# Hash-bucket attention and a mixture of adapters on one core: prologue in another order, adapter work in one pair of heads, one more PSUM copy on ScalarE

## The chip, the cores and the metric

The kernel runs on one core of a Trainium2 chip, as one launch. The metric is the device time of one execution in microseconds (us). TensorE (PE in the rows; PEld is its weight load), VectorE (DVE), ScalarE (ACT), GpSimd (POOL) and SyncE (SP) each work through a queue of their own in order, and wait for one another by semaphores. DMAs are issued by SyncE, ScalarE and GpSimd.

## What is computed

```python
# q, k, v: (4, 8, 768, 64); proj: (64, 6); adapters: E = 8, r = 16; model width 512
q_bucket = sum over bits of ((q @ proj) > 0) * 2**bit      # k_bucket likewise
mask = q_bucket[..., :, None] == k_bucket[..., None, :]
attn = softmax(where(mask, q @ k.T / 8, -1e9))
x = (attn @ v)  arranged as (3072, 512)                    # a batch's 8 heads side by side
logits = x @ w_gate; the two largest per row, softmax over them -> w
out = x + sum over the two: w * ((x @ A[e]) @ B[e])
```

## The kernel before, in words

The 32 heads (4 batches of 8) go by *pairs*: 16 pairs, four to a batch. Partition p holds the six rows 6p to 6p+5 of a head. For a pair, `load` brings Q, K and V; `trans` transposes Q and K of both heads on TensorE in three groups of four 128x128 blocks (`tr{p}_0` to `tr{p}_2`), each followed by one copy out of PSUM into `qkT`; `hash` multiplies `qkT` by the hash vectors (`proj2`, made from the loaded `pst`), VectorE turns the result into signs (`sgn`), and four small DMAs (`sign_dma`) put the signs as six more rows under the casted Q and K in `aug`. So one matmul over 71 rows gives scores in which pairs of different buckets are pushed far down, and no mask is needed. `cast` (VectorE, two calls a pair) fills the other 64 rows of `aug`.

`run` goes through the pairs, and in each through nine *slots*. In slot s, `score` writes 1024 columns of scores into one of two PSUM buffers (pool `ps_s`, two buffers), and ScalarE takes their exponential into `P`. Behind the score each slot has other work on TensorE, written out by hand: probabilities times values (`pvmm`: the second head of the pair before in slots 1 to 3, the first head of this pair in slots 6 to 8), the transposes of coming pairs (group 2 of pair p+1 in slot 0, group 0 of pair p+2 in slot 3, group 1 of pair p+2 in slot 8), the hash of pair p+1 in slot 4, and `xtrans` in slot 7 (transposes of attention outputs `xb` for the adapters). `norm` (VectorE) divides by the sums, for the second head of the pair before in slot 3 and for the first head in slot 0 of the next pair, and frees the one PSUM buffer that `pvmm` writes into (`ps_v`). GpSimd casts V (`vcast`) and the attention outputs (`xb`). SyncE's queue has, per pair, the four sign DMAs (slot 4) and the loads of pair p+3 (slot 5) in this order.

Adapters of a batch start when its four pairs are done, in two halves of three row slots each (`moe_slot`, L432). Before the change a half takes two pairs: in slot 5 of the first the logits and the adapters' first product (`lgz`, TensorE, into the single buffer of `ps_m`) and the gate (`route`: on VectorE three maxima, the differences `d`, the mask `m`; on ScalarE their exponential `e`; on VectorE the weights `gw`, the product `zm`, the sum `ss` and its reciprocal `rt`); in slot 8 the transposes of `zm` and the copy `zmT` (`zmtrans`); and in slots 0, 2 and 3 of the next pair the three outputs (`delta`: one matmul `dl` of 512 columns into `ps_m`, and one VectorE operation that scales it by `rt` and adds `x`). The last half of batch 2 has its gate in pair 14 and its outputs in pair 15.

Pair 15 orders its columns by thirds (`third`), so that its own adapter work can start before all nine slots are done. Behind slot 8 comes the tail: the adapters of batch 3 in groups of two row slots. Every second output there is scaled by ScalarE into `tmp` and added by GpSimd (`split=True`), the others are done by VectorE.

`prologue` (L65) loads pair 0, warms TensorE with 36 matmuls on constants (`warm`), transposes pair 0 by four pieces `trf0` to `trf3`, hashes head 0 (`hsf0`) behind the second piece and head 1 (`hsf1`) behind the fourth, and sends the signs off. `pst` is loaded by two DMAs that ScalarE issues behind its two K loads.

## Time and profile before

| what | us |
|---|---|
| median of 3 runs (205.42 to 207.55) | 207.06 |
| the profiled execution | 207.07 |
| its span | 205.3 |
| ScalarE busy, 181 instructions | 157.3 (77%) |
| TensorE busy, 2177 matmuls | 177.2 (86%) |
| VectorE busy, 277 instructions | 124.7 (61%) |
| GpSimd busy, 107 instructions | 69.7 (34%) |

The span is the time between the first and the last instruction that the profile shows; the execution's time has 1.77 us around it. Busy shares are means over stages with different limits, so the windows of single stages are read beside them. In a row of the timeline the first number is the start, the second the length in us, then engine, line, operation, output and inputs, how often, and in brackets the idle time of the engine just before it and what ended it. Rows of one line that follow each other are merged, with their number behind the x.

### The profile page before, as it was taken

The numbers are of one execution on the slowest core, as the hardware profiler recorded it, in microseconds if no ns is written. First come the engines' busy times: TensorE is split into PE (matmuls) and PEld (weight loads), VectorE is DVE, ScalarE is ACT, GpSimd is POOL, SyncE is SP. The second block draws the span as 40 slices with busy tenths as digits, with TensorE's granted clock in tenths as the row PEclk, the third lists the DMA queues.
The fourth block names the chain that finished last, engine by engine and source line by source line (L and its number), as shares of the span: only waits on it lengthen the run. The fifth ranks groups of instructions, "written<-read, shape, count | busy, mean of one in ns | idle before, by whom it ended". The sixth has DMA issues, their size and how long they took to land.

```text
span 205.3 us, 5283 instructions
## 1 busy us (share of the span) xinstructions
PE 177.2 (86%) x2177; PEld 118.9 (58%) x2177; DVE 124.7 (61%) x277; ACT 157.3 (77%) x181; POOL 69.7 (34%) x107
## 2 busy tenths in 40 slices
...
GB/s 203 257 23 169 101 103 137 47 190 64 181 34 206 59 184 104 138 162 231 20 221 159 232 9 235 157 181 61 210 103 182 135 9 3 160 3 153 22 165 125
DMA packets 20984, 26.37 MB, mean 128 GB/s; under 512 B 6240, under 2 KB 19424, under 8 KB 20960
## 3 DMA queue, kind: packets, MB, share of 16 engines
...
q8 instruction: 17, 0.28, 0.5%
q14 instruction: 7, 0.06, 0.1%
HBM read 19.42 MB, written 6.29 MB: 125 GB/s over the span
## 4 chain that ended last, share of the span: by engine, by line
PE 50%; DVE 21%; issue 9%; ACT 7%; DMA 7%; SPq 2%; POOL 1%; ACTq 1%; POOLq 1%; DVEq 0%
PE s L273 19%; PE pv L280 10%; ACT P L275 6%; DVE qkT L209 6%; PE tr L202 5%; PE hs L222 5%; DVE aug L234 4%; DMA nat<-in_k_dram 4%; DVE x L308 4%; DVE acc L423 3%; DMA pst<-in_proj_dram 3%; PE xtp L348 3%; PE lz L363 2%; PE pv L289 2%; PE hsf L111 2%
## 5 line engine op out<-in xcount | busy, mean ns | idle before, releaser
L275 ACT ACTIVATE P<-s 128x1024 bf16<-128x1024 f32 x144 | 142.5, 1023 | 21.9 <-PE s L273 21.3
L273 PE MATMUL s<-aug 71*128 71x256 bf16 (+1 forms) x396 | 87.0, 326 | 1.0
L280 PEld LDWEIGHTS <-P 128*128 128x128 bf16 x1152 | 48.1, 98 | 11.5 <-issue 0.7
L273 PEld LDWEIGHTS <-aug 71*128 71x128 bf16 x396 | 34.4, 99 | 29.5 <-issue 18.7
L315 POOL CAST xb<-x 128x768 bf16<-128x768 f32 x15 | 12.4, 824 | 108.2 <-DVE x L308 108.2
L280 PE MATMUL pv<-vb,P 128*128 128x65 bf16 x1080 | 48.1, 195 | 0.0
L202 PE MATMUL tr<-ident,nat 128*128 128x128 f32 x180 | 29.0, 280 | 3.5 <-DMA nat<-in_q_dram 1.9
L209 DVE COPY qkT<-tr 128x512 f32<-128x512 f32 x31 | 21.2, 687 | 14.6 <-PE tr L202 14.5
L234 DVE TENSOR_SCALAR aug<-qkT 64x1536 bf16<-64x1536 f32 x30 | 28.6, 952 | 1.2
L202 PEld LDWEIGHTS tr<-ident,nat 128*128 128x128 f32 x180 | 19.9, 140 | 5.7 <-DMA nat<-in_k_dram 2.3
L354 DVE COPY xT<-xtp 128x768 bf16<-128x768 bf16 x15 | 8.4, 558 | 20.7 <-PE xtp L348 20.5
L308 DVE TENSOR_TENSOR x<-pv,ri 128x384 f32<-128x384 f32 x30 | 16.7, 557 | 1.2
L423 DVE SCALAR_TENSOR_TENSOR acc<-dl,rt,x 128x512 f32<-128x512 f32 x21 | 15.7, 745 | 2.5 <-PE dl L415 2.4
L225 DVE TENSOR_SCALAR sgn<-hs 128x384 bf16<-128x384 f32 x15 | 8.4, 558 | 14.1 <-PE hs L222 14.1
L186 POOL TENSOR_TENSOR vs<-vn 128x384 f32<-128x384 f32 x16 | 16.3, 1020 | 0.0
L184 POOL CAST vb<-vn 128x768 bf16<-128x768 f32 x16 | 13.4, 835 | 6.0 <-DMA vn<-in_v_dram 5.9
L415 PE MATMUL dl<-Bcat,zmT 128*128 128x512 bf16 x24 | 9.2, 401 | 5.4 <-DVE acc L423 4.9
L222 PE MATMUL hs<-qkT,proj 128*32 128x384 f32 x120 | 13.4, 521 | 0.0
L289 PE MATMUL pv<-vb,eps 128*128 128x390 bf16 x30 | 10.2, 342 | 2.3 <-DVE x L308 2.3
L207 ACT COPY qkT<-tr 128x512 f32<-128x512 f32 x14 | 8.1, 581 | 3.1 <-PE tr L202 3.1
L348 PE MATMUL xtp<-ident_bf,xb 128*128 128x128 bf16 x96 | 8.3, 219 | 2.5 <-DVE xb L336 1.9
L421 POOL TENSOR_TENSOR acc<-tmp,x 128x512 f32<-128x512 f32 x3 | 3.8, 1263 | 14.5 <-ACT tmp L420 14.5
...
## 6 DMA issues: line engine op xcount, KB each, us to landing
...
aug<-sgn SPq DMA_DIRECT2D x60, 9.0 KB
...
```

The lines of the kernel that those rows point to most:

```text
L186: nc.gpsimd.tensor_add(out=s3, in0=vn[:, :, 0:3, :], in1=vn[:, :, 3:6, :])
L202: nc.tensor.transpose(out=ps[:, j * P:(j + 1) * P], in_=self.nat[p][:, idx % 2, idx // 2, u * P:(u + 1) * P], identity=self.ident)
L209: nc.vector.tensor_copy(out=out, in_=ps)
L222: nc.tensor.matmul(out=ps[32 * j:32 * j + 32, :], lhsT=self.proj2, rhs=self.qkT[p][:, j * 384:(j + 1) * 384], start=True, stop=True)
L234: self.nc.vector.tensor_scalar(out=self.aug[p % 2][0:64, :, e * n:(e + 1) * n], in0=self.qkT[p][64 * e:64 * e + 64, :].rearrange("p (j c) ...
L273: nc.tensor.matmul(out=ps[:, o:o + n], lhsT=aug[0:71, 2 * h + 1, kt * P:(kt + 1) * P], rhs=q, start=True, stop=True)
L275: nc.scalar.activation(out=self.P_[p][:, s * 1024:(s + 1) * 1024], in_=ps, func=ACT.Exp, scale=128.0)
L280: self.nc.tensor.matmul(out=pv, lhsT=self.p_at(p, h, kt, i), rhs=self.vb[p % 3][:, h, self.slot(kt), :], start=False, stop=(last and kt == ...
L289: self.nc.tensor.matmul(out=self.pv[p, h], lhsT=self.eps, start=True, stop=False, rhs=self.vb[p % 3][:, h, self.T, :].unsqueeze(1).to_broa ...
L308: nc.vector.tensor_tensor(out=self.x[b][:, :, c:c + D].rearrange("p (u e) d -> p e u d", e=2), in0=pv[:, :, 0:D].rearrange("p (e u) d -> p ...
L348: nc.tensor.transpose(out=ps[:, i * P:(i + 1) * P], in_=self.xb[b][:, t, hp * P:(hp + 1) * P], identity=self.ident_bf)
L423: nc.vector.scalar_tensor_tensor(out=acc[:, i, :], in0=ps, scalar=rt, in1=x, op0=ALU.mult, op1=ALU.add)
```

## The change

- Prologue: `pst` is loaded by one DMA that reads `proj` twice, and is issued first on ScalarE's queue; the load of V of pair 0 goes behind the loads of pair 1. 38 warm matmuls, then all twelve transposes of pair 0 (into the two buffers of `ps_s`), five more warm matmuls, and then both hashes. All four sign DMAs are issued by SyncE. The first two groups of pair 1's transposes stand in the prologue, behind the hashes and ahead of the first score.
- In every pair the copy of transposes' group 2 (slot 0) is done by ScalarE and not by VectorE, so ScalarE has two such copies per pair (`on_act=True`).
- `moe_slot`: a half of a batch's adapters takes one pair: logits in slot 0, gate in slot 1, `zmtrans` in slot 3, the outputs in slots 5, 6 and 7. Pairs 5, 6, 9, 10, 13 and 14 carry a half each; the other pairs, and pair 15, none of earlier batches.
- Tail: all outputs by VectorE (no `split`), their matmuls into `ps_s`; `route` is cut in two (`route_a` up to `e`, `route_b` from `gw`) so that other work stands between them; two of the copies of `xT` go from ScalarE to VectorE.

```diff
     def prologue(self):
+
+        pst = sg.tile([P, 6], F32, name="pst")
+        nc.scalar.dma_start(out=pst, in_=self.proj.unsqueeze(0).to_broadcast([2, D, 6]))
-        self.load_v(0)
         self.load(1)
-
-        pst = sg.tile([P, 6], F32, name="pst")
-        for e in range(2):
-            nc.scalar.dma_start(out=pst[64 * e:64 * e + 64, :], in_=self.proj)
...
-        self.warm(36)
+        self.load_v(0)
+        self.warm(38)
+        for e in range(2):
+            nc.vector.tensor_copy(out=self.proj2[64 * e:64 * e + 64, e:12:2], in_=pst[64 * e:64 * e + 64, :])
         self.qkT[0] = self.qktp.tile([P, 2 * S], F32, tag="qkT", name="qkT0")
-        for j in range(4):
-            ps = self.ps_t.tile([P, 384], F32, tag="t", name=f"trf{j}")
-            for u in range(3):
...
-                h = j // 2
-                hs = self.ps_t.tile([P, 384], F32, tag="t", name=f"hsf{h}")
-                rows = slice(64 * h, 64 * h + 64)
-                for i in (2 * h, 2 * h + 1):
-                    nc.tensor.matmul(out=hs[32 * i:32 * i + 32, :], lhsT=self.proj2,
-                                     rhs=self.qkT[0][:, i * 384:(i + 1) * 384], start=True, stop=True)
-                sgn = self.sgp.tile([P, 384], BF16, tag="sgn", name=f"sgnf{h}")
...
-                for i in (2 * h, 2 * h + 1):
-                    self.sign_dma(nc.scalar if i == 1 else nc.sync, 0, i, sgn)
+        for h in range(2):
+            ps = self.ps_s.tile([P, 2, 512], F32, tag="s", name=f"trf{h}")
+            for i in range(2):
+                for u in range(3):
+                    nc.tensor.transpose(out=ps[:, i, u * P:(u + 1) * P],
+                                        in_=nat[:, i, h, u * P:(u + 1) * P], identity=self.ident)
+                out = self.qkT[0][:, (2 * h + i) * 384:(2 * h + i + 1) * 384]
+                (nc.scalar.copy if i else nc.vector.tensor_copy)(out=out, in_=ps[:, i, 0:384])
+        self.warm(5)
+        for h in range(2):
+            hs = self.ps_t.tile([P, 384], F32, tag="t", name=f"hsf{h}")
+            rows = slice(64 * h, 64 * h + 64)
+            for i in (2 * h, 2 * h + 1):
+                nc.tensor.matmul(out=hs[32 * i:32 * i + 32, :], lhsT=self.proj2,
+                                 rhs=self.qkT[0][:, i * 384:(i + 1) * 384], start=True, stop=True)
+            sgn = self.sgp.tile([P, 384], BF16, tag="sgn", name=f"sgnf{h}")
+            nc.vector.tensor_scalar(out=sgn[rows], in0=hs[rows], scalar1=0.0, scalar2=0.5,
+                                    op0=ALU.is_gt, op1=ALU.subtract)
+            for i in (2 * h, 2 * h + 1):
+                self.sign_dma(nc.sync, 0, i, sgn)
+            for e in range(2):
+                o = self.aug[0][0:64, 2 * h:2 * h + 2, e * 384:(e + 1) * 384]
+                i_ = self.qkT[0][64 * e:64 * e + 64, h * S:(h + 1) * S].rearrange("p (j c) -> p j c", j=2)
+                if e:
+                    nc.scalar.mul(o, i_, 2.0 ** -5)
+                else:
+                    nc.vector.tensor_scalar(out=o, in0=i_, scalar1=2.0 ** -5, scalar2=None, op0=ALU.mult)
+        self.trans(1, 0)
+        self.trans(1, 1, on_act=True)
...
-    def route(self, b, slots):
-        nc, P, E, r = self.nc, self.P, self.E, self.r
+    def route_a(self, b, slots):
...
         nc.scalar.activation(out=e, in_=d, func=ACT.Exp)
+        self.me[b, slots] = m, e
+
+    def route_b(self, b, slots):
+        nc, P, E, r = self.nc, self.P, self.E, self.r
+        lz, (m, e) = self.lz[b, slots], self.me[b, slots]
...
-        ps = (self.ps_t if last else self.ps_m).tile(
-            [P, self.Dm], F32, tag="t" if last else "m", name=f"dl{b}_{slots[i]}")
+        ps = (self.ps_s if last else self.ps_m).tile(
+            [P, self.Dm], F32, tag="s" if last else "m", name=f"dl{b}_{slots[i]}")
-        rt, x = self.rt[b, slots][:, i:i + 1], self.x[b][:, slots[i], :]
-        if split:
-            tmp = self.xp.tile([P, self.Dm], F32, tag="tmp", name=f"tmp{b}_{slots[i]}")
-            nc.scalar.activation(out=tmp, in_=ps, func=ACT.Copy, scale=rt)
-            nc.gpsimd.tensor_add(out=acc[:, i, :], in0=tmp, in1=x)
-        else:
-            nc.vector.scalar_tensor_tensor(out=acc[:, i, :], in0=ps, scalar=rt, in1=x,
-                                           op0=ALU.mult, op1=ALU.add)
+        nc.vector.scalar_tensor_tensor(out=acc[:, i, :], in0=ps, scalar=self.rt[b, slots][:, i:i + 1],
+                                       in1=self.x[b][:, slots[i], :], op0=ALU.mult, op1=ALU.add)
...
     def moe_slot(self, p, s):
-        for b in range(self.B - 1):
-            first = self.PPB * (b + 1) + 1
-            for g, (r, d) in enumerate(((first, first + 1), (first + 2, first + 3))):
-                if b == self.B - 2 and g == 1:
-                    r, d = r - 1, d - 1
-                slots = tuple(range(3 * g, 3 * g + 3))
-                if p == d and s in (0, 2, 3):
-                    self.delta(b, slots, (0, 2, 3).index(s))
-                if p == r:
-                    if s == 5:
-                        self.lgz(b, slots)
-                        self.route(b, slots)
-                    if s == 8:
-                        self.zmtrans(b, slots)
+        b, g = divmod(p - self.PPB - 1, self.PPB)
+        if b < 0 or b > self.B - 2 or g > 1:
+            return
+        slots = tuple(range(3 * g, 3 * g + 3))
+        if s == 0:
+            self.lgz(b, slots)
+        if s == 1:
+            self.route_a(b, slots)
+            self.route_b(b, slots)
+        if s == 3:
+            self.zmtrans(b, slots)
+        if s in (5, 6, 7):
+            self.delta(b, slots, s - 5)
...
                 if s == 0:
                     if p == 0:
                         self.load(2)
-                        self.trans(1, 0)
                     self.norm(p - 1, 0)
-                    if p > 0:
-                        self.trans(p + 1, 2)
+                    self.trans(p + 1, 2, on_act=True)
                 if s == 1:
                     if p == 0:
-                        self.trans(1, 1)
                         self.load_moe()
                     self.pvmm(p - 1, 1, 0, 2)
-                    if p > 0:
-                        self.cast(p + 1, 0)
+                    self.cast(p + 1, 0)
                     self.vcast(p + 1)
                 if s == 2:
-                    if p == 0:
-                        self.trans(1, 2)
-                        self.cast(1, 0)
                     self.pvmm(p - 1, 1, 2, 5)
                     self.cast(p + 1, 1)
                 if s == 3:
...
-                self.xtrans(p, t[0], last=True)
+                self.xtrans(p, t[0])
...
-                self.xtrans(p, t[1], last=True)
+                self.xtrans(p, t[1])
                 self.zmtrans(b, t[0], last=True)
                 self.third_x(1, self.x[b])
-            self.moe_slot(p, s)
         self.lgz(b, t[1])
-        self.route(b, t[1])
-        self.delta(b, t[0], 0, last=True, split=True)
+        self.route_a(b, t[1])
         self.third(2)
+        self.route_b(b, t[1])
+        self.delta(b, t[0], 0, last=True)
+        self.xtrans(p, t[2], on_act=True)
+        self.lgz(b, t[2])
+        self.zmtrans(b, t[1], last=True)
+        self.third_x(2, self.x[b])
+        self.route_a(b, t[2])
         self.delta(b, t[0], 1, last=True)
-        self.xtrans(p, t[2], last=True)
-        self.zmtrans(b, t[1], last=True)
-        self.lgz(b, t[2])
-        self.third_x(2, self.x[b])
-        self.delta(b, t[1], 0, last=True, split=True)
-        self.route(b, t[2])
+        self.route_b(b, t[2])
+        self.delta(b, t[1], 0, last=True)
+        self.zmtrans(b, t[2], last=True)
         self.delta(b, t[1], 1, last=True)
-        self.zmtrans(b, t[2], last=True)
-        self.delta(b, t[2], 0, last=True, split=True)
-        self.delta(b, t[2], 1, last=True)
+        for i in range(2):
+            self.delta(b, t[2], i, last=True)
```

Three places in the order of the queues. In the names of tiles the first number is the pair (`tr1_0`: pair 1, group 0; `s0_1`: pair 0, slot 1) or, for the adapters' tiles, batch and row slot.

TensorE in the prologue, behind its 36 warm matmuls, before:

```order
L95 MATMUL trf0_162<-ident_107,nat0_90 128x128 x3
L95 MATMUL trf1_169<-ident_107,nat0_90 128x128 x3
L111 MATMUL hsf0_174<-qkT0_161,proj2_112 32x384 x2
L95 MATMUL trf2_183<-ident_107,nat0_90 128x128 x3
L95 MATMUL trf3_188<-ident_107,nat0_90 128x128 x3
L111 MATMUL hsf1_193<-qkT0_161,proj2_112 32x384 x2
L273 LDWEIGHTS aug0_114
L273 MATMUL s0_0_222<-aug0_114 128x512
...
L202 MATMUL tr1_0_233<-ident_107,nat1_97 128x128 x4
```

and with the change, from the last of the first warm matmuls on (of the five others the first stands here):

```order
L153 MATMUL warm_123<-eps_102 128x128
L97 MATMUL trf0_165<-ident_104,nat0_92 128x128 x6
L97 MATMUL trf1_174<-ident_104,nat0_92 128x128 x6
L153 LDWEIGHTS eps_102
L153 MATMUL warm_183<-eps_102 128x128
...
L106 MATMUL hsf0_189<-qkT0_164,proj2_109 32x384 x2
L106 MATMUL hsf1_198<-qkT0_164,proj2_109 32x384 x2
L199 MATMUL tr1_0_208<-ident_104,nat1_97 128x128 x4
L199 MATMUL tr1_1_214<-ident_104,nat1_97 128x128 x4
L270 LDWEIGHTS aug0_111
L270 MATMUL s0_0_240<-aug0_111 128x512
...
L199 MATMUL tr1_2_250<-ident_104,nat1_97 128x128 x4
```

Both hashes have moved behind all transposes of pair 0, and `tr1_0` and `tr1_1` from behind the first scores to ahead of them.

ScalarE in pair 5, the first one with adapter work of batch 0, before:

```order
L275 ACTIVATE P5_1080<-s5_0_1081 128x1024
L275 ACTIVATE P5_1080<-s5_1_1098 128x1024
L275 ACTIVATE P5_1080<-s5_2_1123 128x1024
L275 ACTIVATE P5_1080<-s5_3_1147 128x1024
L207 COPY qkT7_1162<-tr7_0_1163 128x512
L275 ACTIVATE P5_1080<-s5_4_1169 128x1024
L275 ACTIVATE P5_1080<-s5_5_1184 128x1024
L383 ACTIVATE e0_0_1217<-d0_0_1213 128x24
L275 ACTIVATE P5_1080<-s5_6_1225 128x1024
```

and with the change:

```order
L272 ACTIVATE P5_1085<-s5_0_1086 128x1024
L204 COPY qkT6_987<-tr6_2_1097 128x512
L272 ACTIVATE P5_1085<-s5_1_1116 128x1024
L375 ACTIVATE e0_0_1149<-d0_0_1145 128x24
L272 ACTIVATE P5_1085<-s5_2_1159 128x1024
L272 ACTIVATE P5_1085<-s5_3_1183 128x1024
L204 COPY qkT7_1198<-tr7_0_1199 128x512
L272 ACTIVATE P5_1085<-s5_4_1212 128x1024
L272 ACTIVATE P5_1085<-s5_5_1227 128x1024
```

A second copy out of PSUM (`qkT6<-tr6_2`) stands behind exponential 0, and the gate's `e` has moved from behind exponential 5 to behind exponential 1.

VectorE from slot 7 of pair 5 to the last output of batch 0's first half in pair 6, before (`acc0_0` is the sum for row slots 0 to 2):

```order
L354 COPY xT1_1088<-xtp4_0_1260 128x768
L209 COPY qkT7_1162<-tr7_1_1285 128x512
L407 COPY zmT0_0_1295<-ztp0_0_1291 128x384
L306 RECIPROCAL ri5_0_1304<-pv5_0_1230 128x6
L308 TENSOR_TENSOR x1_1086<-pv5_0_1230,ri5_0_1304 128x2x3x64
L209 COPY qkT7_1162<-tr7_2_1307 128x512
L423 SCALAR_TENSOR_TENSOR acc0_0_1297<-dl0_0_1313,rt0_0_1208,x0_375 128x512
L234 TENSOR_SCALAR aug1_115<-qkT7_1162 64x4x384 x2
L423 SCALAR_TENSOR_TENSOR acc0_0_1297<-dl0_1_1365,rt0_0_1208,x0_375 128x512
L306 RECIPROCAL ri5_1_1379<-pv5_1_1320 128x6
L308 TENSOR_TENSOR x1_1086<-pv5_1_1320,ri5_1_1379 128x2x3x64
L423 SCALAR_TENSOR_TENSOR acc0_0_1297<-dl0_2_1390,rt0_0_1208,x0_375 128x512
```

and in pair 6 with the change, where the second half of batch 0 has gate and outputs in one pair:

```order
L231 TENSOR_SCALAR aug1_112<-qkT7_1198 64x4x384
L367 MAX top0_3_1366<-lz0_3_1328 128x8 x3
L369 TENSOR_TENSOR d0_3_1370<-lz0_3_1328,top0_3_1366 128x24
L372 TENSOR_TENSOR m0_3_1372<-lz0_3_1328,top0_3_1366 128x24
L385 TENSOR_TENSOR gw0_3_1378<-m0_3_1372,e0_3_1374 128x24
L386 TENSOR_TENSOR zm0_3_1376<-lz0_3_1328,gw0_3_1378 128x384
...
L231 TENSOR_SCALAR aug1_112<-qkT7_1198 64x4x384
...
L305 TENSOR_TENSOR x1_1091<-pv5_1_1345,ri5_1_1419 128x2x3x64
L407 COPY zmT0_3_1434<-ztp0_3_1430 128x384
L222 TENSOR_SCALAR sgn7_1446<-hs7_1441 128x384
L417 SCALAR_TENSOR_TENSOR acc0_3_1436<-dl0_3_1462,rt0_3_1377,x0_380 128x512
...
L347 COPY xT1_1093<-xtp5_0_1503 128x768
```

The gate stands between the two casts, the copy `zmT` ahead of the signs `sgn7`, and the sums `acc` behind them; the copy of `tr8_2` has left this queue.

## Rows read from the trace of the kernel before

**Rows 1.** Windows: busy PE, PEld, DVE, ACT, POOL, clock, DMA share, GB/s.

```profile
15.55:30.28 14.73, 12.11 (x91) 6.92 (x90) 6.01 (x9) 9.48 (x10) 5.70 (x8) 0.77 0.50 117
30.28:70.61 40.33, 38.47 (x499) 25.87 (x498) 22.67 (x41) 36.96 (x40) 13.94 (x20) 1.00 0.35 115
40.11:49.81 9.70, 9.42 (x127) 6.44 (x125) 5.63 (x11) 9.20 (x10) 3.47 (x5) 1.00 0.38 127
70.61:157.19 86.58, 81.71 (x1067) 56.27 (x1065) 60.66 (x133) 75.21 (x85) 27.76 (x40) 1.00 0.44 150
178.95:190.46 11.51, 9.30 (x145) 7.32 (x145) 7.00 (x21) 9.29 (x12) 0.83 (x1) 1.00 0.17 70
190.46:205.30 14.84, 4.87 (x52) 2.41 (x50) 6.65 (x22) 3.93 (x11) 3.79 (x3) 0.68 0.29 108
```

**Rows 2.** Timeline of the start, from the hash vectors to the first exponential.

```profile
1.68 1.19 ACTq L77 DMA_DIRECT2D pst<-in_proj_dram  x2
...
4.74 0.82 PE L95 MATMUL trf<-ident,nat 128*128 128x128 f32 x6
...
8.43 0.61 DVE L104 COPY proj<-pst 64x6 f32<-64x6 f32 x1 [1.63 <-DMA pst<-in_proj_dram]
...
9.19 1.49 PE L111 MATMUL hsf<-qkT,proj 128*32 128x384 f32 x4 [3.63 <-DVE proj L104]
...
10.73 0.55 DVE L114 TENSOR_SCALAR sgnf<-hsf 64x384 bf16<-64x384 f32 x1 [1.69 <-PE hsf L111]
...
11.31 1.64 ACTq L139 DMA_DIRECT2D aug<-sgnf  x1
...
14.91 0.33 PEld L273 LDWEIGHTS <-aug 71*128 71x128 bf16 x3 [1.20 <-DMA aug<-sgnf]
...
15.55 2.85 ACT L275 ACTIVATE P<-s 128x1024 bf16<-128x1024 f32 x3 [1.21 <-PE s L273]
```

**Rows 3.** Window of 1 us in the start, columns as in rows 1.

```profile
8.00:9.00 1.00, 0.00 (x0) 0.00 (x0) 0.57 (x1) 0.00 (x0) 1.00 (x2) 0.50 0.93 349
```

**Rows 4.** Timeline of pair 0, TensorE at the transposes of pair 2.

```profile
20.54 0.52 PE L202 MATMUL tr<-ident,nat 128*128 128x128 f32 x3 [1.89 <-DMA nat<-in_q_dram]
```

**Rows 5.** Chain of waits (start, us, what): a load of pair 2, logits in pair 9.

```profile
17.73 3.72 DMA nat<-in_k_dram
...
119.47 0.71 PE lz L363 x12
```

**Rows 6.** Timeline of an undisturbed pair, ScalarE, VectorE, TensorE at score 6.

```profile
40.11 1.94 ACT L275 ACTIVATE P<-s 128x1024 bf16<-128x1024 f32 x2 [0.31 <-PE s L273]
...
41.71 1.92 DVE L234 TENSOR_SCALAR aug<-qkT 64x1536 bf16<-64x1536 f32 x2
...
42.24 2.01 ACT L275 ACTIVATE P<-s 128x1024 bf16<-128x1024 f32 x2 [0.19 <-PE s L273]
...
44.15 0.58 ACT L207 COPY qkT<-tr 128x512 f32<-128x512 f32 x1
...
45.71 0.31 PEld L273 LDWEIGHTS <-aug 71*128 71x128 bf16 x2 [0.39 <-issue]
```

**Rows 7.** Timeline of pairs 9 and 10: gate and outputs of a half.

```profile
120.79 0.22 ACT L383 ACTIVATE e<-d 128x24 f32<-128x24 f32 x1 [0.26 <-DVE d L377]
...
122.01 0.18 DVE L392 RECIPROCAL rt<-ss 128x3 f32<-128x3 f32 x1
...
129.72 0.74 DVE L423 SCALAR_TENSOR_TENSOR acc<-dl,rt,x 128x512 f32<-128x512 f32 x1
```

**Rows 8.** Timeline of the tail.

```profile
192.03 0.18 DVE L385 TENSOR_TENSOR gw<-m,e 128x16 f32<-128x16 f32 x1 [0.20 <-ACT e L383]
...
196.21 1.26 POOL L421 TENSOR_TENSOR acc<-tmp,x 128x512 f32<-128x512 f32 x1 [2.29 <-ACT tmp L420]
196.27 1.23 DVE L385 TENSOR_TENSOR gw<-m,e 128x16 f32<-128x16 f32 x1 [0.67 <-ACT e L383]
...
200.39 1.26 POOL L421 TENSOR_TENSOR acc<-tmp,x 128x512 f32<-128x512 f32 x1 [2.92 <-ACT tmp L420]
```

51 lines of the change are left out of this document (15 added, 36 removed).

## The prediction

> **What bounds the kernel now.** I read the windows by stage first, then the timeline of each stage, and the chain of waits for what ends last in it. The windows [rows 1] split the run into a start (up to the first exponential at 15.55), pair 0, four pairs without adapter work, eight pairs with it, pairs 13 and 14 (157.19 to 178.95), the last pair, and a tail behind the last exponential. In an undisturbed pair (40.11 to 49.81) ScalarE is busy 9.20 of 9.70 us with nine exponentials and one copy, and TensorE 9.42: both are nearly full, and neither can be lengthened for nothing. The start and pair 0 are different: 15.55 and 14.73 us, with TensorE at a mean clock of 0.77 in pair 0. That is where idle time lies.
>
> The start [rows 2] is one chain. `pst`, the hash vectors, is issued last on ScalarE's queue (1.68); VectorE can take its second half only at 8.43; TensorE waits 3.63 us for it and then hashes the first head for 1.49 us; the signs are ready at 11.28 (10.73 + 0.55), their DMA lands for the score at 14.91, and the first exponential starts at 15.55. Meanwhile the clock has fallen to 1.2 GHz, half of full speed [rows 3], after TensorE had done nothing from 5.56 on. Pair 0 then waits 1.89 us for the Q rows of pair 2 [rows 4] and for its K rows until 21.45 [rows 5], since SyncE issues their loads only behind the signs (17.73).
>
> **The change, part by part.**
>
> *Start.* `pst` becomes the first DMA on its queue, 0.9 us ahead of its row in [rows 2], with no K rows in front. All twelve transposes stand behind 38 warm matmuls: 36 ended at 4.74, two more take 0.2; six transposes took 0.82, twelve take 1.65; five more warm matmuls 0.5. The hash starts near 7.1. At full clock the first head's 1.49 halves to 0.75, then 0.1 to VectorE and 0.55 for the signs: 8.6. From signs to score I keep what the rows show, 14.91 - 11.28 = 3.63, although both sign DMAs now stand on SyncE one behind the other (the row of ScalarE's has 1.64 for its issue alone, two on SyncE should be no more). Score at 12.2, first exponential 0.64 later, 12.85: a gain of 2.7. The two transposes of pair 1 that now stand ahead of the score lie in the 3.6 us in which it waits for signs; they cost nothing unless that wait gets shorter than about 1.2 us. V of pair 0 lands behind pair 1's rows now, about 2 us later, and GpSimd's casts and its DMAs of the adapters' weights with it; slot 6 of pair 0 is the first to need V, some 6 us behind the first score, so I cost that at nothing.
>
> *Pair 0.* Its bounds are the undisturbed 9.70 from below and 14.73 less the wait for Q, 12.8, from above. The load of pair 2 is issued behind the four signs, near 11.5 and 12.0; its K rows took 3.7 us [rows 5], so 15.7, and slot 3 needs them near 12.85 + 3.1: no slack, but no longer late by more than the wait that is there now. TensorE has little to do from about 8.8 to 12.2, as before the fall in [rows 3], so I expect 1.2 GHz for part of this pair. ScalarE hides most of that, since TensorE has no earlier pair's second half to do here. I take 10.8, nearer the lower bound. Pair 1 starts at 23.65 and not at 30.28: **-6.6**.
>
> *The second copy on ScalarE.* The transposes' third group is copied behind exponential 0, by ScalarE. VectorE's casts waited for VectorE's own copy and began at 41.71; they now wait for ScalarE's, which ends at the same point, 40.11 + 0.97 + 0.58 (two exponentials take 1.94, the copy that is there now 0.58 [rows 6]). So VectorE wins nothing on the path. ScalarE loses about 0.47: nine exponentials at 0.97 are 8.73, with the copy 9.20 [rows 1]. Of its two idle pieces, 0.31 ahead of exponential 0 and 0.19 ahead of exponential 2 [rows 6], the second is absorbed, so exponential 2 is 0.28 later. The first can't be: score 6 waits for the buffer that exponential 4 frees (45.71 [rows 6]), and from there it is 4.1 us to the next pair's first exponential (49.81), all of it TensorE's queue. The pair becomes 9.70 + 0.28, about 10.0. Bounds: 9.67 if both pieces vanish (9.20 + 0.47), 10.28 if neither does. The hash and its signs are late by the same 0.28, behind exponential 2. The first four pairs take 40.33 now, mean 10.08, 1.5 us in all over four undisturbed ones; at 10.0 to 10.3 each they cost 40.0 to 41.2. I take **+0.4**.
>
> *Adapters in one pair.* What two pairs shared (logits and gate in one, outputs in the next) stands in one; of each four pairs two carry it and two have none. TensorE's floor: the eight pairs have 81.71 busy, 10.21 each, against 9.42 without; 0.79 for a half, so 11.0 for both. Upwards, by the order on VectorE, counted from exponential 0: a cast (+1.6 to +2.56, half of the row of 1.92 in [rows 6]) stands ahead of the gate, whose head to `e` takes 0.61 (logits' end at 119.47 + 0.71 [rows 5] to 120.79 [rows 7]). So `e` starts at +3.1 to +3.2; ScalarE, ready for exponential 2 at +2.41, stops 0.65 and does `e`, with 0.13 net 0.78 late. In [rows 7] it stops 0.26 for the same thing. The logits (0.71) sit in the slack behind score 0. The first output waits for `zmT`: from `e` the gate takes 1.40 [rows 7], the other cast 0.96, the second normalisation and `zmT`'s copy about 1.1, so +6.5; exponential 4 ends at +6.6, so score 6 is no later for it. Two outputs stand behind score 6: 512 columns each, 0.22 by the logits' 1632 columns in 0.71, +0.44. Sum 10.0 + 0.78 + 0.44, about 11.2; I take 11.3. VectorE's three sums of 0.74 [rows 7] fit, but the signs are queued behind `zmT` (7.1, landing near 10.5, needed at 10.9): 0.4 of cover. If that is gone each adapter pair is longer by what it is late; upper bound 12.0. Four pairs: 2 x 11.3 + 2 x 10.0 = 42.6 against 43.29; twice: **-1.4**. Pairs 13 and 14 both carry adapters now: 11.3 + 10.85 (14 has one group of transposes less, 0.44) against 21.76: **+0.4**.
>
> *Last pair.* Three outputs of 0.22 leave TensorE's queue, for which ScalarE waits there (9.29 busy of 11.51 [rows 1]): **-0.6**.
>
> *Tail.* In [rows 8] a product of 16 elements takes 1.23 us and ends where GpSimd's addition ends (197.5); the one before it took 0.18. Without GpSimd's additions that is 1.05 back. VectorE now does all six outputs. Following its order from the last exponential's end: last third's values at +2.4, gate to +3.4, output +4.15, third +4.55, gate's head +5.15, output +5.9, gate +6.9, four outputs of 0.74 to +9.9; two copies of `xT` are among it and delay nothing that ends last; now the last addition ends at 201.65, +11.2 [rows 8]. **-1.3**; if TensorE's clock (a mean of 0.68 in the tail) delays the last two outputs, nothing is won.
>
> Sum: -6.6 + 0.4 - 1.4 + 0.4 - 0.6 - 1.3 = -9.1. The profiled execution took 207.07 (span 205.3), the median of the runs shown is 207.06. 207.07 - 9.1 = **198.0**.
>
> **Rivals.** *pst late (0.20).* In [rows 2] its second DMA took 6.1 us from its issue (2.3) to its use. If it takes that again it lands at 6.9, and VectorE's two `pst` copies stand ahead of its Q copies: Q is ready near 8.3, the hash 1.2 later, the K rows queued behind `pst` late as well, and TensorE idles longer, so pair 0 at 1.2 GHz: +1.3. Together 200.5. For it: the new DMA reads `proj` twice by a leading stride of zero. The Trainium skill, DMA: Bandwidth & Descriptors, Rules for kernel authors, says that a leading zero-stride broadcast of c copies confines a DMA to c engines, here two of sixteen; no run here shows it yet, and by that rule 200.5 would be the forecast. Against it: only 3 KB, and up to 6.0 it is covered.
>
> *Adapter pairs at 12.0 (0.16).* Signs or `zmT` late on VectorE: six pairs x 0.7 = 4.2, 202.2. For it: VectorE is busy some 8.9 of 11.3 in such a pair (5.63 plain, 60.66 / 8 with a half [rows 1], less the copy). Against it: 0.4 of cover.
>
> *Better (0.12).* Pair 0 at 10.0, and plain pairs at 9.7 (eight x 0.3): 194.8. For it: ScalarE is idle 0.5 in a plain pair. Against it: the chain from score 6.
>
> *Slower (0.05).* The clock falls inside the loop. ScalarE's longer pairs leave TensorE idle more. A pair of 9.42 busy would need 18.8 at 1.2 GHz, +9.1: one such pair ends the gain, one and a half give 211. Against it: the clock is 1.00 in all loop rows of [rows 1], in the last with TensorE busy 9.30 of 11.51.
>
> **How the numbers follow.** My forecast has 0.47, its own range 196 to 199.5. The range of 194.0 to 202.5 leaves out the slower case and the two middle ones together or past their prices. About 1% (2 us) is what a measurement of this kernel tells from no change. Faster by more: forecast, better, and each middle rival alone, less their joint cases, 0.89. Within 1%: late `pst` with long adapter pairs, 0.06. Slower: 0.05.
>
> **What would show it.** Right: the first exponential near 12.85; pair 1 near 23.6; one copy behind exponential 0, and pairs of 10.0 without adapter work, with no idle ahead of exponential 2; 11.3 in pairs 5, 6, 9, 10, 13; a wait of about 0.6 of ScalarE for `d`; no product over 0.3 in the tail. Wrong: VectorE waiting for `pst` past 6; scores waiting for signs in adapter pairs; a clock under 1.00 behind pair 1; first scores of pair 0 still waiting for pair 2's rows.

## The result, and the profile after

The changed kernel takes 199.19 us (median of 4 runs, 196.94 to 200.13) against 207.31 (205.42 to 207.86): a ratio of 0.9588, 95% interval 0.9476 to 0.9699. It is faster, by 8.1 us, and 1.2 us from the forecast of 198.0. Ratios here and below leave out executions more than 1.5% above the fastest of their kernel on that chip, so they are not the quotients of the medians, and the profiled execution of the change (200.13) is one of those left out. The sum behind the forecast, however, is wrong in almost every term. The profiled execution has a span of 198.0, 7.3 less than before; what it shows of the start holds for this execution, and p1_old_prologue below has the other three. By stages, in us, with starts read from ScalarE's timeline (in a merged row of exponentials the last one starts 1.02 ahead of the row's end):

| stage | before | after | change | forecast |
|---|---|---|---|---|
| start, to the first exponential | 15.55 | 16.62 | +1.07 | -2.7 |
| pair 0 | 14.73 | 14.74 | 0.0 | -3.9 |
| pairs 1 to 4 | 40.33 | 39.29 | -1.04 | +0.4 |
| pairs 5 to 12 | 86.58 | 83.31 | -3.27 | -1.4 |
| pairs 13, 14 | 21.71 | 21.66 | -0.05 | +0.4 |
| last pair | 11.56 | 10.56 | -1.0 | -0.6 |
| tail | 14.82 | 11.77 | -3.05 | -1.3 |

The windows of after, with the columns of [rows 1] and answering to them (start and pair 0; pairs 1 to 4; a pair without adapters; pairs 5 to 12; the last pair; the tail):

```profile
16.62:31.36 14.74, 14.06 (x83) 7.89 (x82) 3.15 (x4) 10.05 (x11) 9.22 (x12) 1.00 0.96 146
31.36:70.65 39.29, 37.96 (x499) 25.73 (x498) 20.20 (x37) 37.88 (x44) 13.85 (x20) 1.00 0.34 110
31.36:41.15 9.79, 9.45 (x127) 6.47 (x126) 5.11 (x10) 9.47 (x12) 3.47 (x5) 1.00 0.18 60
70.65:153.96 83.31, 81.27 (x1067) 55.89 (x1065) 55.62 (x125) 77.20 (x93) 27.78 (x40) 1.00 0.47 156
175.62:186.18 10.56, 8.57 (x142) 7.02 (x142) 4.91 (x19) 9.11 (x12) 0.83 (x1) 1.00 0.20 78
186.18:198.00 11.82, 5.30 (x52) 2.42 (x50) 7.93 (x27) 1.85 (x6) 0.00 (x0) 0.71 0.36 133
```

VectorE has 5 us less to do in pairs 5 to 12 (60.66 to 55.62), ScalarE 2 us more. In the first row the clock column reads 1.00, but this can't be so, as the rows of pair 0 below show: the trace's first record of the clock is at 30.7, and ahead of it the view fills in full speed.

The K loads of pair 0 on ScalarE's queue, before:

```profile
0.75 0.90 ACTq L71 DMA_DIRECT2D nat<-in_k_dram  x2
```

The start of after, from the issue of `pst` to the first exponential (timeline, answering to [rows 2]):

```profile
0.74 1.15 ACTq L69 DMA_DIRECT2D pst<-in_proj_dram  x1
...
1.92 0.84 ACTq L74 DMA_DIRECT2D nat<-in_k_dram  x2
...
4.08 1.46 DVE L91 COPY proj<-pst 64x6 f32<-64x6 f32 x2 [1.32 <-DMA pst<-in_proj_dram]
...
5.08 0.85 PE L97 MATMUL trf<-ident,nat 128*128 128x128 f32 x3
...
5.97 0.56 DVE L100 COPY qkT<-trf 128x384 f32<-128x384 f32 x1 [0.42 <-PE trf L97]
6.61 1.28 ACT L100 ACT_TABLE_LOAD   x1 [6.61 <-DVE qkT L100]
6.90 1.14 PEld L97 LDWEIGHTS trf<-ident,nat 128*128 128x128 f32 x6 [1.37 <-DVE qkT L100]
6.93 1.51 PE L97 MATMUL trf<-ident,nat 128*128 128x128 f32 x6 [1.00 <-DMA nat<-in_k_dram]
...
9.10 0.90 PE L97 MATMUL trf<-ident,nat 128*128 128x128 f32 x3 [0.65 <-DVE qkT L100]
...
10.46 1.59 PE L106 MATMUL hsf<-qkT,proj 128*32 128x384 f32 x8
...
12.61 3.37 SPq L136 DMA_DIRECT2D aug<-sgnf  x4
...
16.62 1.02 ACT L272 ACTIVATE P<-s 128x1024 bf16<-128x1024 f32 x1 [1.07 <-PE s L270]
```

`pst` is there by 4.08, so the hash no longer waits for it. But the twelve transposes don't run in a row. K's three wait for VectorE to have copied Q's three, since both lie in one PSUM tile (`trf0`, `trf1`), and for their rows, which are there at 6.93 only (before, the six transposes from 4.74 on had them without a wait): `pst`, 1.15 us to issue, now stands ahead of them on ScalarE's queue, so that they leave at 1.92 and not at 0.75. Of the fourteen traces of this document the six with the old order have no such wait, the eight with the new order all have one (0.67 to 2.40); what `pst` and the other loads that changed places each do to it was not tried. ScalarE's table load, which stood at 2.9 in the old order, now stands behind the same copy (6.61). And six transposes take 1.51 us, not 0.82. The hashes start at 10.46, where the prediction had 7.1.

Pair 0 of after on TensorE, and the same operation behind it (timeline):

```profile
21.48 0.48 PE L199 MATMUL tr<-ident,nat 128*128 128x128 f32 x1 [0.42 <-DMA nat<-in_k_dram]
...
22.73 1.51 PE L219 MATMUL hs<-qkT,proj 128*32 128x384 f32 x8
...
26.18 0.87 PE L277 MATMUL pv<-vb,P 128*128 128x65 bf16 x12
...
32.55 0.53 PE L277 MATMUL pv<-vb,P 128*128 128x65 bf16 x12
```

Twelve products take 0.87 us in pair 0 and 0.53 in pair 1, and the eight hash matmuls 1.51 against 0.85 (at 45.24): TensorE ran at 1.2 GHz through the start and pair 0, up to about 30 us, when the trace's first clock record says 1.00. K rows of pair 2 are still waited for (21.48).

ScalarE in a pair without adapters, and in pair 5, which holds a whole half (timeline of after, answering to [rows 6] and [rows 7]):

```profile
41.15 1.02 ACT L272 ACTIVATE P<-s 128x1024 bf16<-128x1024 f32 x1 [0.31 <-PE s L270]
...
42.07 0.58 ACT L204 COPY qkT<-tr 128x512 f32<-128x512 f32 x1
...
42.53 2.88 ACT L272 ACTIVATE P<-s 128x1024 bf16<-128x1024 f32 x3
...
45.25 0.63 ACT L204 COPY qkT<-tr 128x512 f32<-128x512 f32 x1
...
45.72 4.91 ACT L272 ACTIVATE P<-s 128x1024 bf16<-128x1024 f32 x5
...
73.61 0.22 ACT L375 ACTIVATE e<-d 128x24 f32<-128x24 f32 x1 [0.42 <-DVE d L369]
...
80.37 1.02 ACT L272 ACTIVATE P<-s 128x1024 bf16<-128x1024 f32 x1 [0.33 <-PE s L270]
```

The copy starts 0.92 behind exponential 0, whose row says 1.02, and exponential 1 starts 0.46 behind the copy, whose row says 0.58: what follows directly starts some 0.1 before the row ahead of it ends. The three exponentials take 2.72 up to the second copy. Exponential 4 starts 4.57 behind exponential 0; before it was 4.50 (40.11 to 44.61). The pair takes 9.79, the pair with a half 11.05.

The tail of after (timeline, answering to [rows 8]):

```profile
191.20 0.17 DVE L385 TENSOR_TENSOR gw<-m,e 128x16 f32<-128x16 f32 x1
...
192.02 2.90 DVE L417 SCALAR_TENSOR_TENSOR acc<-dl,rt,x 128x512 f32<-128x512 f32 x4
```

No product of 16 elements takes 1.23 us any more. The last output is written at 194.92, 8.74 behind the last exponential's end (before 11.2), and the span ends 3.0 later (before 3.65).

### The profile page after: what moved, and what is told of

It reads as the page before. It is cut to its first block, busy times and chain, and to the rows that moved or that the text cites. A ratio compares the mean times of both kernels' runs of the same rounds, so it can differ in the third digit from the quotient of the medians.

```text
span 198.0 us, 5277 instructions
## 1 busy us (share of the span) xinstructions
PE 180.7 (91%) x2184; PEld 122.2 (62%) x2184; DVE 116.5 (59%) x266; ACT 159.7 (81%) x192; POOL 66.8 (34%) x104
## 4 chain that ended last, share of the span: by engine, by line
PE 48%; DVE 20%; ACT 12%; DMA 7%; issue 6%; SPq 2%; ACTq 1%; POOLq 0%; POOL 0%; DVEq 0%
PE s L270 17%; PE pv L277 12%; ACT P L272 9%; DMA nat<-in_k_dram 7%; PE tr L199 6%; DVE aug L231 5%; ACT qkT L204 3%; DVE qkT L206 3%; DVE x L305 3%; PE pv L286 3%; PE xtp L345 3%; DVE zm L386 2%; PE dl L415 2%; DVE acc L417 2%; SPq L136 2%
## 5 line engine op out<-in xcount | busy, mean ns | idle before, releaser
L270 PE MATMUL s<-aug 71*128 71x256 bf16 (+1 forms) x396 | 89.9, 333 | 2.5 <-ACT P L272 1.8
L277 PEld LDWEIGHTS <-P 128*128 128x128 bf16 x1152 | 48.5, 99 | 11.6 <-issue 1.0
L199 PE MATMUL tr<-ident,nat 128*128 128x128 f32 x180 | 30.9, 294 | 1.1 <-DVE sgnf L109 0.6
L199 PEld LDWEIGHTS tr<-ident,nat 128*128 128x128 f32 x180 | 21.4, 149 | 4.0 <-DVE sgnf L109 2.3
L347 DVE COPY xT<-xtp 128x768 bf16<-128x768 bf16 (+1 forms) x17 | 8.9, 526 | 24.0 <-PE xtp L345 24.0
L204 ACT COPY qkT<-tr 128x512 f32<-128x512 f32 x30 | 17.9, 596 | 3.4 <-PE tr L199 3.4
L417 DVE SCALAR_TENSOR_TENSOR acc<-dl,rt,x 128x512 f32<-128x512 f32 x24 | 17.9, 748 | 2.9 <-PE dl L415 2.8
L206 DVE COPY qkT<-tr 128x512 f32<-128x512 f32 x15 | 10.4, 692 | 13.1 <-PE tr L199 13.1
L181 POOL CAST vb<-vn 128x768 bf16<-128x768 f32 x16 | 13.3, 830 | 5.5 <-DMA vn<-in_v_dram 4.9
L222 DVE TENSOR_SCALAR sgn<-hs 128x384 bf16<-128x384 f32 x15 | 8.3, 553 | 11.2 <-PE hs L219 11.2
L415 PE MATMUL dl<-Bcat,zmT 128*128 128x512 bf16 x24 | 9.8, 409 | 1.1 <-ACT zmT L405 0.2
L185 POOL TENSOR_TENSOR vs<-vs 128x128 f32<-128x128 f32 x16 | 7.6, 476 | 1.3
```

What stands on the lines that cost most here:

```text
L199: nc.tensor.transpose(out=ps[:, j * P:(j + 1) * P], in_=self.nat[p][:, idx % 2, idx // 2, u * P:(u + 1) * P], identity=self.ident)
L204: nc.scalar.copy(out=out, in_=ps)
L206: nc.vector.tensor_copy(out=out, in_=ps)
L270: nc.tensor.matmul(out=ps[:, o:o + n], lhsT=aug[0:71, 2 * h + 1, kt * P:(kt + 1) * P], rhs=q, start=True, stop=True)
L277: self.nc.tensor.matmul(out=pv, lhsT=self.p_at(p, h, kt, i), rhs=self.vb[p % 3][:, h, self.slot(kt), :], start=False, stop=(last and kt == ...
L417: nc.vector.scalar_tensor_tensor(out=acc[:, i, :], in0=ps, scalar=self.rt[b, slots][:, i:i + 1], in1=self.x[b][:, slots[i], :], op0=ALU.mu ...
```

## The experiments

**Theory:** the gain comes from the loop and the tail alone; the new prologue gives nothing, since its transposes wait for PSUM tiles and TensorE runs at 1.2 GHz. **Rival:** the prologue gives its 6.6 us and one unlucky profile hides it. Within the loop: either placement or ScalarE's copy carries the gain. The stages of each kernel's profiled execution, in us, read as above; the last column is the median of its runs, and in brackets that of the kernel before on the same chip:

| kernel | start | pair 0 | 1-4 | 5-12 | 13, 14 | last | tail | median |
|---|---|---|---|---|---|---|---|---|
| before | 15.55 | 14.73 | 40.33 | 86.58 | 21.71 | 11.56 | 14.82 | 207.31 |
| after | 16.62 | 14.74 | 39.29 | 83.31 | 21.66 | 10.56 | 11.77 | 199.19 (207.31) |
| p1_old_prologue | 14.79 | 14.88 | 39.20 | 83.31 | 21.67 | 10.56 | 11.92 | 199.60 (206.94) |
| p2_adapters | 14.49 | 16.51 | 39.42 | 83.86 | 21.87 | 10.92 | 15.61 | 203.39 (206.94) |
| p3_act_copy | 13.33 | 17.84 | 39.56 | 84.25 | 21.12 | 11.56 | 14.83 | 203.81 (206.94) |
| p4_tail | 13.68 | 16.88 | 39.36 | 87.29 | 21.73 | 11.21 | 11.70 | 203.63 (206.94) |
| p5_free | 15.47 | 13.56 | 39.14 | 84.24 | 22.07 | 10.56 | 11.74 | 197.46 (207.65) |
| p6_loads | 17.23 | 12.98 | 40.92 | 83.74 | 21.67 | 10.56 | 11.77 | 200.29 (207.65) |
| p7_keep | 15.25 | 15.05 | 39.43 | 91.54 | 22.42 | 10.56 | 11.74 | 204.53 (207.65) |
| p8_start | 13.88 | 9.46 | 40.67 | 86.42 | 22.34 | 10.56 | 11.76 | 199.10 (207.65) |
| p9_start_early | 13.81 | 9.46 | 39.16 | 83.34 | 21.67 | 10.56 | 11.99 | 192.10 (206.14) |
| p10_early | 15.49 | 14.28 | 39.15 | 83.32 | 21.67 | 10.56 | 11.88 | 197.70 (206.14) |
| p12_before_early | 15.05 | 14.78 | 38.92 | 86.17 | 21.72 | 11.56 | 14.84 | 205.60 (206.14) |
| p11_no_keep | 14.84 | 9.46 | 39.47 | 83.31 | 21.67 | 10.57 | 11.99 | 193.89 (206.51) |

Where no load is late, pairs 5 to 12 repeat within 0.05 us from kernel to kernel with the changed loop (83.31 to 83.34 in five traces) and within 0.4 with that of before (86.58 and 86.17), so what one part does there can be read from single traces. The start and pair 0 don't repeat: with one and the same prologue (before, p1 to p4) their sum lies between 29.67 and 31.18, the first exponential alone between 13.33 and 15.55. Single executions scatter more: those of the kernel before lie between 202.25 and 208.52 on one chip.

**p1_old_prologue**, the change without its prologue:

```diff
-        (prologue of the changed kernel; trans(1, 0) and trans(1, 1) in it)
+        (prologue of the kernel before; trans(1, 0..2) in slots 0, 1, 2 of pair 0)
```

> The changed kernel with the prologue of before and the transposes of pair 1 back in the slots of pair 0; all else as changed. Theory (the new prologue gives nothing: first exponential 16.62 against 15.55 us, pair 0 14.74 against 14.73): the first exponential starts at 15.5 to 15.6 us, exponential 0 of pair 1 at 30.3, and the time is about 1 us below the changed kernel's median of 199.2, so about 198.1. Rival (the new prologue does give its 6.6 us wherever TensorE runs at full speed early, and the profiled execution only did not show it): 203 to 205.5 us.

Measured: 199.60 us (198.1 to 200.42), ratio to before 0.9696 (0.9567 to 0.9825); first exponential 14.79, exponential 0 of pair 1 at 29.67. Everything behind that point takes 166.65 us, in the changed kernel 166.59. If that part is as long in the other runs, which no trace shows, their spans give their start and pair 0 as an estimate: 30.3, 32.0 and 32.0 here (spans 197.0, 198.6, 198.6), 28.2, 30.1 and 30.7 for the changed kernel (194.8, 196.7, 197.3). So in the mean of four (30.1 against 31.0) the new prologue gives 0.9 us, less than the runs scatter, and not 6.6. The rival, 203 us or more, falls; the theory's 198.1 isn't met either.

**p2_adapters, p3_act_copy, p4_tail**, each one part of the change in the kernel before:

```diff
 # p2_adapters: moe_slot of the changed kernel, none in the last pair
+        b, g = divmod(p - self.PPB - 1, self.PPB)
...
+        if s in (5, 6, 7):
+            self.delta(b, slots, s - 5)
 # p3_act_copy
-                        self.trans(p + 1, 2)
+                        self.trans(p + 1, 2, on_act=True)
 # p4_tail: xtrans, route_a / route_b, delta and the tail of the changed kernel
-        self.delta(b, t[0], 0, last=True, split=True)
+        self.route_a(b, t[1])
         self.third(2)
+        self.route_b(b, t[1])
+        self.delta(b, t[0], 0, last=True)
```

> The kernel before, with only the adapter outputs moved (a whole group in one pair, none in the last pair). Theory (by the stages, where the pairs without adapters already give 0.26 us each by the copy alone): pairs 5 to 12 lose 3.27 - 8 x 0.26 = 1.2 us, pairs 13 and 14 gain 0.45, the last pair loses 0.7: together -1.4, about 205.9 us from 207.3. Rival (the whole gain of pairs 5 to 12 and of the last pair is the placement's): -3.3 - 1.0 = -4.3, about 203.

> The kernel before, with only the third transposed piece of each pair from pair 1 on copied out of PSUM by ScalarE in place of VectorE. Theory (pairs 1 to 4 hold no adapters in either kernel and became 0.26 us shorter each): 14 pairs x 0.26 = -3.6, about 203.7 us from 207.3; the gap ahead of exponential 2 of a pair is gone, and 0.58 us of copy takes its place on ScalarE, overlapped so that exponential 4 starts at most 0.1 later. Rival (the term of the prediction: the copy costs about 0.1 us a pair more than it frees): 207.5 to 208.5.

> The kernel before, with only what the change does to the last pair's own adapters and behind the last exponential (no GpSimd additions, copies of xT on VectorE, the route in two halves, outputs from the two-bank PSUM pool); adapters of the batch before stay in the last pair. Theory (tail 14.84 to 11.83 us): -3.0 in the tail, nothing or up to 0.3 more in the last pair, about 204.2 us from 207.3; no multiplication gw takes 1.2 us any more. Rival (the shorter tail needs the last pair to be free of the others' adapters, whose outputs occupy VectorE ahead of the route): -1 to -1.5 only, about 206.

Measured: 203.39, 203.81 and 203.63 us against 206.94; the ratios 0.9890 (0.9774 to 1.0006), 0.9895 (0.9749 to 1.0041) and 0.9892 (0.9782 to 1.0002) each reach to about 1, so the stages have to tell. (The time of p2_adapters is its rival's; that of p3_act_copy is its theory's, but not by 0.26 us in every pair, as the stages show.) The tail edits, which were run only together, are worth what the theory said: 14.82 to 11.70, with the others' adapters still in the last pair. The other two are not: each takes 2.3 to 2.7 us off pairs 5 to 12, both together 3.3. They save the same time. Pairs 5 to 8, in which these traces (p12_before_early for the kernel before) show no wait for rows, make it plain: 43.06 before (10.28, 11.25, 10.28, 11.25 in p12_before_early), 41.65 with the placement alone (11.10, 11.11, 9.70, 9.74), 42.04 with the copy alone (10.28, 10.65, 10.46, 10.65), 41.66 with both. Once the adapters are placed, the copy on ScalarE gives nothing. The waits of TensorE in pairs 5 to 8 (us in total, times, longest) show what the two have in common, in p12_before_early (told further down; its loop is that of before but for when loads are issued) first and in p3_act_copy second; in p2_adapters there is no such row:

```profile
PE dl L415 <- DVE acc L423: 1.7, 2, 0.9
```

```profile
PE dl L415 <- DVE acc L423: 0.6, 2, 0.3
```

and ScalarE's exponential 4 in pair 6, in the kernel before and in p3_act_copy (timelines):

```profile
86.64 1.02 ACT L275 ACTIVATE P<-s 128x1024 bf16<-128x1024 f32 x1 [0.84 <-PE s L273]
```

```profile
86.17 1.02 ACT L275 ACTIVATE P<-s 128x1024 bf16<-128x1024 f32 x1 [0.24 <-PE s L273]
```

In a pair with outputs, the third output's matmul (slot 3) waits for VectorE to empty the one `ps_m` buffer, and VectorE has a normalisation, the copy of the transposes and two casts ahead of that; the scores stand behind the matmul on TensorE, and ScalarE loses 0.84. Taking the copy from VectorE shortens this wait, and taking the outputs out of slots 0 to 3 ends it. In pairs without adapters the copy gives nothing: 38.92 for four of them in p12_before_early, 39.15 in p10_early.

**p5_free, p6_loads, p7_keep**, one suspect of the start each, in the changed kernel:

```diff
 # p5_free: a PSUM tile per piece, hashes in ps_v and ps_m, the table early
+        nc.scalar.activation(out=first, in_=self.eps[:, 0:1], func=ACT.Exp)
...
-            ps = self.ps_s.tile([P, 2, 512], F32, tag="s", name=f"trf{h}")
+                ps = (self.ps_t.tile([P, 512], F32, tag="t", name=f"trf{h}{i}") if h
+                      else self.ps_s.tile([P, 1024], F32, tag="s", name=f"trf{h}{i}"))
 # p6_loads
         self.load_v(0)
+        self.load(2)
...
-                    if p == 0:
+                    if p == 2:
                         self.load_moe()
 # p7_keep
-        self.warm(5)
+                self.warm(8)      # behind each of the four pieces
...
+        self.warm(20)             # behind trans(1, 1)
```

> The changed kernel with a PSUM tile of its own for each of the four transposed pieces of pair 0 (the hashes in two others), and one small exponential on ScalarE behind its DMA issues, so that the table is loaded early. Theory (the K transposes wait for VectorE's copy of the Q half of the same tile, and the copies for the table): the table load stands near 3 us in place of 6.61, the last transposes of head 1 at about 8.5 in place of 9.10 to 10.0, the hashes at 9.5 in place of 10.46, the first exponential at 15.6 in place of 16.62; time about 198.2 against 199.2. Rival (the landing of the K rows sets the start, 6.93 and later): no change, 199.2.

> The changed kernel with the loads of pair 2 issued in the prologue, ahead of the sign DMAs, and the adapters' weights loaded in pair 2 in place of pair 0. Theory (pair 0 waits for pair 2's K rows, 0.42 on PE and 0.82 on its weight loads, and shares the DMA engines with the weights' 4800 small packets): the wait at 21.48 is gone, pair 0 takes 13.3 to 13.8 us in place of 14.74, time about 198. Rival (1.2 MB more ahead of the sign DMAs hold these up): the sign DMAs land 1 to 2 us later, the first exponential at 17.5 to 18.5, time 199 to 200.

> The changed kernel with 8 more small matmuls behind each of the four transposed pieces (in place of 5 behind all) and 20 behind the transposes of pair 1, while TensorE waits for the sign DMAs. Theory (pair 0 takes 14.7 us because its scores run at half rate, 1.04 in place of 0.60 us each, and TensorE's idle time ahead of it is why): the first exponentials' scores take 0.60, pair 0 12 us or less in place of 14.74, time about 196.5. Rival (what TensorE does in these gaps does not move the granted clock, or the added matmuls only stand in the way): pair 0 14.7, first exponential 0 to 1 us later, time 199 to 200.5.

p5_free: 197.46 us (196.2 to 198.77), ratio 0.9692 (0.9526 to 0.9857). The table load stands at 2.80, nine transposes run in a row, the hashes start at 9.64 and the first exponential at 15.47, 1.15 earlier (timeline):

```profile
2.80 1.28 ACT L80 ACT_TABLE_LOAD   x1 [2.80 <-issue]
...
7.00 2.18 PE L100 MATMUL trf<-ident,nat 128*128 128x128 f32 x9 [1.07 <-DMA nat<-in_k_dram]
...
15.47 1.02 ACT L275 ACTIVATE P<-s 128x1024 bf16<-128x1024 f32 x1 [2.96 <-PE s L273]
```

The theory's number came out, but it doesn't show the theory. p10_early below has after's prologue unchanged, and its trace reads:

```profile
6.50 0.85 PE L97 MATMUL trf<-ident,nat 128*128 128x128 f32 x6 [1.04 <-DMA nat<-in_k_dram]
...
15.49 1.02 ACT L272 ACTIVATE P<-s 128x1024 bf16<-128x1024 f32 x1 [0.50 <-PE s L270]
```

There six transposes take 0.85 and not 1.51, with the clock recorded as 1.00 from 4.8 to 8.2, and the first exponential is as early with the shared tiles and the late table. So 1.1 us is also what two executions of one prologue differ by, and what the tile and the table are worth is not shown apart from that. The K rows are there at 7.0 in any case, which the rival had right.

p6_loads: 200.29 us (199.79 to 201.07), ratio 0.9822 (0.9641 to 1.0002). Pair 0 takes 12.98, shorter than the theory's 13.3 to 13.8, but the K rows of pair 0 come at 7.67 (6.93 in after), the first exponential starts at 17.23, 0.6 later, and pair 2, which now has the adapters' weights, takes 11.44 in place of 9.79. By these two traces the loads of pair 2 and the weights cost pair 0 1.8 us; moved alone, they cost it elsewhere.

p7_keep: 204.53 us, its runs 197.93 to 208.2; too far apart for a ratio. The added matmuls do hold the clock, for a while: its record is 1.00 from 6.2 to 19.8, the eight hash matmuls take 1.02 at 10.10 (1.59 in after), and the first exponential starts at 15.25, 1.4 earlier. But from 16 to 19.8 TensorE has little to do and then waits for Q and K rows of pair 2 (0.30 and 0.79), the clock is 0.50 from there to 30.1, and pair 0 takes 15.05: not the theory's 12, and near the rival's 14.7, but not for its reason, since the added matmuls did move the clock. Here the clock fell in a stretch of waits, the last of them for loads, so clock and loads hang together. What makes this execution slow is the same thing again in pair 7 (timeline of TensorE, and the windows' row of the stretch behind, columns of [rows 1]):

```profile
98.85 0.47 PE L200 MATMUL tr<-ident,nat 128*128 128x128 f32 x1 [2.67 <-DMA nat<-in_k_dram]
...
100.10 1.51 PE L220 MATMUL hs<-qkT,proj 128*32 128x384 f32 x8
```

```profile
101.00:108.60 7.60, 7.60 (x62) 5.14 (x59) 1.11 (x2) 4.22 (x5) 1.67 (x3) 0.50 0.27 87
```

TensorE waited 2.67 us for K rows, and its clock was 0.50 from 98.3 to 108.6: pair 7 took 16.84 us, 7.05 more than its 9.79, of which the wait is the smaller part.

**p8_start**, all three together, with head 0 first:

```diff
+            # for each head: transposes, warm(6), hash, signs, their DMAs, then the next head
+        self.warm(12)              # behind trans(1, 1)
```

> The changed kernel with the three edits together (own PSUM tiles and early table, early loads of pair 2 and late adapter weights, 6 + 6 + 12 small matmuls) and head 0's hashes and sign DMAs ahead of head 1's transposes. Theory (each piece of the start costs what the rows show): first exponential at 13 us, pair 0 in 12, exponential 0 of pair 1 at 25 in place of 31.36, all else as in the changed kernel; time about 193.5. Rival (the DMA engines, busy at 300 GB/s and more from 3 to 13 us, set the start, whatever the order on TensorE): exponential 0 of pair 1 at 29 to 31, time 197 to 199.

Measured: 199.10 us (196.44 to 204.74), ratio 0.9656 (0.9342 to 0.9969), first exponential 13.88, pair 0 9.46, exponential 0 of pair 1 at 23.33: the start and pair 0 are 8.0 us shorter, better than the theory's 25, and the clock is 1.00 from its first record at 4.1 on. The time, however, is that of the rival, since pairs 1 to 14 take 149.4 in place of 144.3. TensorE's waits from pair 1 to the last pair (us in total, times, longest):

```profile
PE tr L203 <- DMA nat<-in_k_dram: 4.8, 6, 1.2
```

The K rows of coming pairs land after TensorE wants them. On SyncE their loads stand behind four sign DMAs (3.1 us to issue) and leave 8.7 to 11.2 us into the pair. In after they stand in the same place and leave 8.8 to 10.4 us into it (from pair 1 on) with no such wait; why they land later here no run shows.

**p9_start_early, p10_early, p12_before_early**: p8_start, the changed kernel and the kernel before, each with one edit:

```diff
                 if s == 0:
+                    self.load(p + 3)
                     self.norm(p - 1, 0)
...
-                if s == 5:
-                    self.load(p + 3)
```

> The kernel p8_start with the loads of pair p + 3 issued in slot 0 of pair p in place of slot 5 (where they stand on SP behind four sign DMAs, 3.1 us, and leave at 8.8 to 9.9 us into the pair). Theory (p8's start is 8.0 us shorter, 23.33 against 31.36, and it loses 5.2 of it again because the K rows land after PE wants them: 4.8 us in six waits): no wait for K rows in the loop, pairs of 9.8 and 11.05 throughout, exponential 0 of pair 1 at 23 to 25, time 191.5 to 194. Rival (the loop's slower pairs come from the faster start in another way, so that K rows merely end last): time 196 to 199 as p8.

> The changed kernel with only the loads of pair p + 3 in slot 0. Theory (in the profile of the changed kernel no pair from 1 on waits for K rows, so there is nothing to gain but runs in which they happen to be late): pairs as in the changed kernel's profile, exponential 0 of pair 1 at 28 to 31.5, time 196.5 to 199. Rival (six loads at once in pair 0 hold up the signs of pair 1): pair 0 or 1 longer by 1 us or more, time 200.

> The kernel before with only the loads of pair p + 3 in slot 0. Theory (before's pairs 1 to 4 took 40.33 us where the same code takes 39.36 in p4_tail, because K rows were late once, 0.86 us; the 1.04 us that the change seems to gain there are such waits): pairs 1 to 4 take 39.3, pairs 5 to 14 as before (10.35 and 11.25 each), time 205 to 206.5 against 207. Rival (late K rows are also what the adapter pairs lost): pairs 5 to 12 at 84.5 or less, time 203 or less.

Measured: **192.10 us** for p9_start_early (191.77 to 196.1), a ratio of 0.9288 (0.9232 to 0.9344) to before: faster than the changed kernel's 0.9588 (0.9476 to 0.9699), with intervals apart. No wait for K rows is left, and the loop is the changed kernel's to 0.1 us. The loads leave between 1.0 us ahead of a pair's exponential 0 and 0.4 behind it, behind the sign DMAs of the pair before: five slots in the program are some 10 us on the queue. Its pair 0 on ScalarE (timeline):

```profile
13.81 1.02 ACT L276 ACTIVATE P<-s 128x1024 bf16<-128x1024 f32 x1 [0.69 <-PE s L274]
...
18.39 5.91 ACT L276 ACTIVATE P<-s 128x1024 bf16<-128x1024 f32 x6
```

The last row runs into pair 1 without a gap that the view shows; after's had eight gaps from exponential 0 of pair 0 to that of pair 1.

p10_early: 197.70 us (195.97 to 199.99), ratio 0.9509 (0.9430 to 0.9587), as the theory said; against the changed kernel's own runs no difference can be told. So the early loads alone don't give p9_start_early its time. p12_before_early: 205.60 (201.45 to 206.65) against 206.14. Its windows (pairs 1 to 4, pairs 5 to 12; columns of [rows 1]):

```profile
29.83:68.75 38.92, 37.74 (x499) 25.83 (x498) 22.66 (x41) 36.81 (x40) 13.90 (x20) 1.00 0.36 121
68.75:154.93 86.18, 81.33 (x1067) 56.33 (x1065) 61.00 (x133) 75.15 (x85) 27.76 (x40) 1.00 0.44 151
```

Pairs 1 to 4 take 1.4 us less than in the profile of before, with the same work in them. So what the change seems to gain there is no gain of its edits; 0.86 us of it is one wait for late K rows in pair 4 of before, and for the rest the view shows no wait:

```profile
64.32 0.33 PE L202 MATMUL tr<-ident,nat 128*128 128x128 f32 x1 [0.86 <-DMA nat<-in_k_dram]
```

The rival falls: pairs 5 to 12 keep 86.2.

**p11_no_keep**, p9_start_early without its small matmuls:

```diff
-            self.warm(6 if h == 0 else 6)
...
-        self.warm(12)
```

> The kernel p9_start_early without its 6 + 6 + 12 small matmuls in the start (the 38 ahead of the first transposes stay). Theory A (TensorE's work in these gaps is why its clock stayed at 2.4 GHz from 4.6 us on and pair 0 took 9.46 us): the granted clock falls to 0.50 for some of the first 30 us, pair 0 takes 11.5 to 14 us, time 194.5 to 197. Theory B (the shorter gaps of the new order alone do it): pair 0 again at 9.5, first exponential up to 0.6 us earlier, time 191.5 to 192.5.

Measured: 193.89 us (192.01 to 196.64), ratio 0.9367 (0.9274 to 0.9460), an interval that overlaps p9_start_early's. The clock falls to 0.50 only from 8.2 to 11.6, the first exponential is 1.0 later (14.84), and pair 0 takes 9.46 again. TensorE had waited 1.86 us for K rows ahead of the fall, and head 0's hash then takes 2.13 us where p8_start has 1.14 (timeline):

```profile
7.32 0.55 PE L101 MATMUL trf<-ident,nat 128*128 128x128 f32 x3 [1.86 <-DMA nat<-in_k_dram]
...
7.79 2.13 PE L108 MATMUL hsf<-qkT,proj 128*32 128x384 f32 x4
```

So pair 0 is as theory B says; the time lies between the two theories' ranges. Of the 1.0 in the start, 0.4 is K rows that come later than in p9_start_early (7.32 against 6.90), so by these two traces the small matmuls are worth some 0.6. Own PSUM tiles alone, early loads alone and small matmuls alone each left pair 0 with a clock of 0.50 in it; which of the tiles, the loads and the new order of the heads would do was not tried.

## Why the prediction was right in time and wrong in its sum

*Start and pair 0: wrong by 7.7 us in the profiled execution (4.6 to 7.1 by the estimate for the other three).* The steps that failed: "all twelve transposes in a row, 1.65", and "at full clock the first head's 1.49 halves to 0.75". The first had K's rows on time, though they are issued 1.17 later, behind `pst` (only the rival on `pst` has them "late as well"): they land at 6.9, in no trace with the new order ahead of 6.5. It also overlooked that Q's and K's transposes share a PSUM tile that VectorE still reads. The second overlooked that TensorE could still be at 1.2 GHz: the hashes took 1.59. At full clock a head's hash does take 0.84 (p3_act_copy, where before has 1.49). The steps from signs to score (3.63 forecast, 2.96 measured, 12.58 to 15.54) and for `pst` were sound; the two transposes of pair 1 did lie in the wait for the signs. Exponential 0 of pair 1 was forecast at 23.65, and p8_start and p9_start_early, with a shorter start in other ways, reach 23.33 and 23.27; that they come so close is chance, 13.88 and 9.46 in place of 12.85 and 10.8. For pair 0, 10.8 stood nearer to the lower bound on the ground that ScalarE hides a slow TensorE. It doesn't: pair 0 took 12.98 to 17.84 in every trace with TensorE at 1.2 GHz in it (the 12.98 with the loads of pair 2 out of its way), 9.46 in the three without.

*Rivals.* "`pst` late" did not come: `pst` landed 3.3 us after its issue (0.74 to 4.08). The Trainium skill, DMA: Bandwidth & Descriptors, Rules for kernel authors, says that a leading broadcast of two copies confines a DMA to at most two engines; for 3 KB no delay shows here, so the trace neither bears it out nor speaks against it. "Slower", a fall of the clock inside the loop, did not come in the changed kernel, but p7_keep shows it, near its price: +7.05 for a pair (forecast +9.1 for a whole pair at 1.2 GHz). "Adapter pairs at 12.0" did not come (11.04); of "better" the plain pairs nearly did (9.79), pair 0 did not.

*The second copy: mechanism right, size wrong.* The chain from exponential 4 to the next pair is as told, and the gap of 0.31 stayed. But the pair grows by 0.09 (9.70 to 9.79), not 0.28. The term took 0.97 for an exponential, half of the merged row of two in [rows 6] (1.94), but such a row is one distance of 0.92 and one length of 1.02. So the gap of 0.19 in brackets was worth 0.29 from start to start, and exponentials 2 and 3, a row of 2.01, stood 0.99 apart and hid 0.07 more. 0.36 of the copy's 0.46 lies in idle time that it ends. The Trainium skill, ScalarE: Activation LUTs, What ACT_TABLE_LOAD costs, says that ACTIVATEs (the exponentials) back to back overlap by about 93 ns; the trace agrees (1.02 against 0.92). By this alone 14 pairs came out about 3 us too long: 10.0 against 9.79, 11.3 against 11.04. The difference between a pair with and one without a half was right, 1.3 against 1.25. In pairs 1 to 4 the sign of +0.4 was right as well, against an undisturbed before (38.92 to 39.15); the -1.04 comes from the profile of before, with 0.86 of late K rows in it.

*Adapters.* "ScalarE stops 0.65 and does `e`" was 0.42; `zmT` and the first output were early enough (76.93, forecast +6.5, measured +6.28). That both edits relieve the same wait on VectorE, the prediction did not see; it had the copy as a loss and the placement as a small gain.

*Last pair:* -0.6 forecast, -1.0 measured: the placement gives 0.64 (10.92), and 0.35 comes from the last pair's own copies of `xT` on VectorE (11.21), which were costed at nothing.

*Tail:* the cause was right (no product over 0.3, GpSimd's additions gone), the size not: -3.05 against -1.3. The order on VectorE was forecast step by step from the lengths of rows, +9.9; measured +8.74, since the operations overlap, each step 0.1 to 0.2 shorter than forecast (a gate took 0.82 and not 1.0). The remaining 0.6 is the end behind the last output, 3.0 in place of 3.65.

So against the profiled execution the forecast stood 7.7 us too low in the start and about 6 too high behind it. That the total came out is the two cancelling, not the sum's merit.
